# One head's value product in one slot, row sums divided out after it, and casts on GpSimd, in a bucketed attention followed by a gated convolution layer

## The chip, the cores and the metric

The kernel runs on one core of one Trainium2 chip. The core has five engines that run side by side and wait for each other through semaphores: TensorE (PE in the profile; its weight loads are PEld), VectorE (DVE), ScalarE (ACT), GpSimd (POOL), and SyncE (SP), which here only issues DMAs. The metric is the device time of one execution in microseconds (us); lower is better.

## The reference

There are B = 4 batches of H = 8 heads, each with S = 768 positions of D = 64 numbers, in float32. Every query and key gets a bucket number from the signs of six projections; a query sees only keys of its own bucket.

```python
q_bits = (einsum('bhsd,dk->bhsk', q, proj) > 0)          # six bits; the same for k
mask   = q_bucket[:, :, :, None] == k_bucket[:, :, None, :]
scores = where(mask, matmul(q, k.T) / sqrt(D), -1e9)
attn   = exp(scores - max(scores)); attn = attn / (sum(attn) + 1e-9)
x      = matmul(attn, v)                                  # heads side by side: (B, S, 512)
gate   = sigmoid(sum_k conv_w[k] * x shifted by 4-k)      # causal, five taps, per channel
out    = (gate * (x @ w_val)) @ w_out
```

`w_val`, `conv_w` and `w_out` arrive as float64, and the kernel turns their bits into float32 pairs itself.

## The kernel before, in words

**Units, tiles, slots.** A unit is one head of one batch (32 units). A tile is 128 queries of a unit against all 768 keys (6 per unit, N = 192 in all). The main loop (L453) takes one tile forward per turn; a turn is called a slot here, k. The order of every engine's instructions is written out by hand: inside `manual_schedule`, PE, ACT, DVE and POOL run exactly the order in which the loop emits them. Only SP's order of DMA issues is left to a planner. All engines are first in, first out: an instruction that waits holds everything behind it on its engine.

**Slot k.** ACT copies the transposed tile k-4 out of PSUM (`keep_transposed`, L289, two copies). DVE takes the row maxima of tile k from PSUM (L238) and makes two small factors from them (L244, L248). Between these, in every second slot, DVE adds 1e-9 to the row sums of tiles k-2 and k-1 and takes their reciprocals (L262, L266); POOL multiplies tile k-2 with them (`normalise`, L271). PE computes the scores of tile k+1 (L232, four matmuls into one of two PSUM buffers). ACT takes the exponential of tile k (L256) and adds up its rows on the way. Then come pieces of other work, each a Python generator that is moved one step at a time: `convs` (the gate's convolution), `weights` (float64 to float32 pairs, mostly DVE, over the first nine units or so), `moes` (the two matrix products of the last layer), `preps` (operands of the unit after next) and `avs` (attention times values). Last, PE transposes tile k-3 (L280; LAG = 3). A score buffer is free for tile k+2 once the exponential of tile k has read it.

**Value product.** When the sixth tile of a unit has been copied, `attn_v` is ready: 12 matmuls (six key blocks, two halves of the queries), whose 64 output columns use one half of the PE array each, so the two halves run at the same time. Every odd slot takes two steps of it, so four matmuls; the trace shows each float32 matmul as two records, so such a run is `x8`. A unit has three runs, in three slots. Its result is copied by ACT into `x` (L311). After every second head `pair_x` splits `x` into a rounded part and a rest (L323 on DVE, L324 on POOL) and runs the five taps on DVE (L332 once, L334 four times). After a batch's last pair ACT applies the sigmoid (L338) and `moe` of that batch is appended: eight `val` chunks and six `outp` chunks of three steps (four matmuls) each, two empty steps, and a `hold` before the last two `outp`, which stay until the next batch's gates are there. A `val` chunk's result is multiplied with the gate on DVE straight after its last matmul (L370) and split (L374 on DVE, L376 on POOL); an `outp` chunk's result is copied and stored (L396 or L398, L400). Both read the one PSUM buffer `m` that the next chunk fills.

**Preparation.** `prep` rounds a raw unit to fp32r on DVE (L166), POOL forms the rest (L168), and seven DMAs on SP lay out the stacked operands (L169 to L175) and load a later unit (L147); `bits` (L194, L197) makes the bucket rows for four units at a time.

Of the kernel before, what the change touches and what calls it, by code (L numbers as in the profile page):

```python
# [26 lines left out]
def kernel(  # L27
# [12 lines left out]
    P = 128  # L40
# [5 lines left out]
    LAG = 3  # L46
# [8 lines left out]
    pp = ctx.enter_context(tc.tile_pool(name="pp", bufs=LAG + 1))  # L55
# [7 lines left out]
    op = ctx.enter_context(tc.tile_pool(name="op", bufs=2))  # L63

# [92 lines left out]
    def prep(i):  # L157
# [8 lines left out]
        nc.vector.tensor_copy(out=aq, in_=r)  # L166
# [83 lines left out]
    def exponentials(k):  # L250
        s, nb = ss.pop(k), nbs.pop(k)
        p = pp.tile([P, 2, HS], FP32, name="p")
        if k % 2 == 0:
            cur["sm"] = small.tile([P, 2, 2], FP32, name="sm")
        sm = cur["sm"]
        nc.scalar.activation(out=p, in_=s[:, :, 0:HS], func=AF.Exp, bias=nb, scale=gs.pop(k), accum_out=sm[:, k % 2, 0:1])  # L256
        ps[k] = (p.rearrange("p a b -> p (a b)"), sm)


    def row_sums(k):  # L260
        sums[k] = small.tile([P, 2, 2], FP32, name="s1")
        nc.vector.tensor_scalar(out=sums[k][:, :, 0], in0=ps[k][1][:, :, 0], scalar1=1e-9, scalar2=None, op0=ALU.add)  # L262

    def recip(k):
        ri = small.tile([P, 2], FP32, name="ri")
        nc.vector.reciprocal(out=ri, in_=sums.pop(k)[:, :, 0])  # L266
        rcs[k], rcs[k + 1] = ri[:, 0:1], ri[:, 1:2]

    def normalise(k):
        p, _ = ps[k]  # L270
        nc.gpsimd.tensor_scalar(out=p, in0=p, scalar1=rcs.pop(k), scalar2=1.0, op0=ALU.mult, op1=ALU.mult)  # L271

    def transposes(k):
        p, _ = ps.pop(k)
# [19 lines left out]
    def attn_v(i, pts):  # L294
# [4 lines left out]
        for kb in range(KB):  # L299
            if kb:  # L300
                yield
            for s, pt in enumerate(pts):
                nc.tensor.matmul(out=av[s * D:(s + 1) * D, 0:HS], lhsT=vt[:, kb, hh * D:(hh + 1) * D], rhs=pt[kb // 3][:, kb % 3, :],  # L303
                                 start=(kb == 0), stop=(kb == KB - 1), tile_position=(0, s * D))
        if hh == 0:
            x = cur["x"] = xp.tile([P, S + KW - 1], FP32, name="x")
            nc.gpsimd.memset(x[:, 0:KW - 1], 0.0)
        x = cur["x"]
        for s in range(2):
            o = KW - 1 + s * HS  # L310
            nc.scalar.copy(out=x[hh * D:(hh + 1) * D, o:o + HS], in_=av[s * D:(s + 1) * D, 0:HS])  # L311
        if hh == 1:
            if c == 0:
                cur["xs"], cur["g"] = {}, []
            convs.append(pair_x(b, c, x, cur["g"], cur["xs"]))

    def pair_x(b, c, x, gs, xs_):
        for o in (0, HS):
# [4 lines left out]
            nc.vector.tensor_copy(out=xh, in_=x0)  # L323
            nc.gpsimd.tensor_tensor(out=xl, in0=x0, in1=xh.bitcast(FP32), op=ALU.subtract)  # L324
        yield
        g = gp.tile([P, S], FP32, name="g")
        gs.append(g)
        for k in range(KW):
            yield
            w = cw_sb[:, c * KW + k:c * KW + k + 1]  # L330
            if k == 0:
                nc.vector.tensor_scalar(out=g, in0=x[:, 0:S], scalar1=w, scalar2=None, op0=ALU.mult)  # L332
            else:
                nc.vector.scalar_tensor_tensor(out=g, in0=x[:, k:k + S], scalar=w, in1=g, op0=ALU.mult, op1=ALU.add)  # L334
        if c == NP - 1:
# [14 lines left out]
    def moe(b, xs_, g):  # L350
# [3 lines left out]
        def later():  # L354
            while todo:
                todo.pop(0)()

        def val(o, j):
# [11 lines left out]
            nc.vector.tensor_tensor(out=ht, in0=acc[:, 0:HS], in1=g[j][:, o:o + HS], op=ALU.mult)  # L370
# [10 lines left out]
        def outp(o, tb):  # L381
# [4 lines left out]
            for hi, wi in ((0, 0), (0, 1), (1, 0)):  # L386
# [6 lines left out]
                later()  # L393
            ob = op.tile([P, 512], FP32, name="o")
# [29 lines left out]
    raws, stacks, vts, ss, nbs, ps, tps, sums, rcs, nms, gs, cur = {}, {}, {}, {}, {}, {}, {}, {}, {}, {}, {}, {}  # L424
    avs, convs, moes = [], [], []
# [9 lines left out]

    def finish(gens):
# [120 lines left out]
```

## Time and profile before

| | before |
|---|---|
| median of 3 runs (lowest, highest) | 639.28 us (639.07, 639.45) |
| the profiled execution's own time | 637.56 us |
| its span in the trace | 635.6 us |
| granted PE clock, mean | 0.989 |
| busy: PE, DVE, ACT, POOL | 590.1, 465.9, 421.7, 364.7 us |
| main loop's last value product ends, by the chain of waits | about 589.4 us |
| first sigmoid of the gates (L338) starts | 196.3 us |

The page gives the busy time of each engine, groups of instructions with their mean duration, and the chain of work that ended last, followed backwards. On that chain a piece's length is the time by which it moved the end, which for pipelined matmuls is shorter than the duration of the record itself. A row of the stage table reads: window, its length, then busy time (and count) of PE, PEld, DVE, ACT and POOL, granted PE clock, DMA share and GB/s.

### The profile page before, as it was taken

Reading aid. Unit: us, or ns where it says so; the run is one execution under the profiler, and the core shown is the slowest. Engines: PE = TensorE matmul, PEld = TensorE weight load, DVE = VectorE, ACT = ScalarE, POOL = GpSimd, SP = SyncE. Lnnn points to the kernel's source line nnn. Section 1 sums busy time; section 2 is a strip of 40 time slices with the busy share of each in tenths; the row PEclk is TensorE's granted clock in tenths of the full one; section 3 lists DMA queues with packets and bytes.
Section 4 is the critical chain, followed back from the end, with each engine's and each line's share of the span. In section 5 each row is a group of like instructions: output and inputs, shape, how many; then the busy total and the mean of one; then the engine's idle time right before and its main releaser. Section 6 shows DMA issues by size and latency. Waiting matters only on the chain.

```text
span 635.6 us, 10630 instructions
## 1 busy us (share of the span) xinstructions
PE 590.1 (93%) x3496; PEld 424.3 (67%) x3496; DVE 465.9 (73%) x1064; ACT 421.7 (66%) x881; POOL 364.7 (57%) x326
## 2 busy tenths in 40 slices
PE   4689888878999999999999999999999999999997
PEld 2465554555567777676667877677667777776895
DVE  5789897999986766668675877578685787665532
ACT  3487776767778666667787766677778677675400
POOL 1375868577765764567653776466562677544221
PEclk9899998998999999999999999999999999999999
DMA  6533535443332334343433333343422223300111
GB/s 243 128 101 86 139 96 138 112 134 81 104 80 58 83 75 123 82 105 96 104 80 79 88 80 110 80 121 80 120 57 61 57 53 79 86 18 2 50 51 50
DMA packets 23269, 56.76 MB, mean 89 GB/s; under 512 B 4296, under 2 KB 4296, under 8 KB 23216
## 3 DMA queue, kind: packets, MB, share of 16 engines
q1 hardware_dynamic: 23072, 56.06, 32.9%
q8 instruction: 28, 0.46, 0.3%
q14 instruction: 25, 0.20, 0.1%
q10 hardware_dynamic: 144, 0.03, 0.0%
HBM read 23.12 MB, written 6.29 MB: 46 GB/s over the span
## 4 chain that ended last, share of the span: by engine, by line
PE 64%; DVE 18%; ACT 10%; issue 3%; DMA 3%; POOL 0%; DVEq 0%; ACTq 0%
PE av L303 16%; PE s L232 15%; PE tp L280 12%; PE m L390 8%; PE m L365 7%; DVE nm L238 6%; ACT p L256 4%; DVE g L334 3%; ACT pt L289 3%; ACT x L311 2%; DMA w<-in_w_out_dram 2%; DVE aq L166 1%; PE tp L365 1%; PE tp L390 1%; PE s L390 1%
## 5 line engine op out<-in xcount | busy, mean ns | idle before, releaser
L271 POOL TENSOR_SCALAR p<-p,ri 128x768 f32<-128x768 f32 x192 | 220.0, 1150 | 200.3 <-DVE nb L248 157.6
L256 ACT ACTIVATE p<-s,nb,gs 128x768 f32<-128x768 f32 x192 | 192.7, 1004 | 49.7 <-DVE nb L248 44.6
L289 ACT COPY pt<-tp 128x384 f32<-128x384 f32 x384 | 166.2, 485 | 86.0 <-PE tp L280 85.0
L238 DVE TENSOR_REDUCE nm<-s 128x1 f32<-128x768 f32 x192 | 182.4, 950 | 52.8 <-PE s L232 52.6
L280 PEld LDWEIGHTS tp<-ident,p 128*128 128x128 f32 x1152 | 130.4, 142 | 74.2 <-issue 47.3
L280 PE MATMUL tp<-ident,p 128*128 128x128 f32 x1152 | 165.4, 280 | 4.5 <-ACT pt L289 1.6
L232 PE MATMUL s<-ak,aq 76*128 76x384 f32 x384 | 118.6, 390 | 32.2 <-ACT p L256 25.4
L303 PE MATMUL av<-pt,vt 128*64 128x384 f32 x768 | 146.9, 504 | 0.0
L232 PE MATMUL s<-bk,bq 128*128 128x384 f32 x384 | 101.6, 346 | 0.0
L232 PEld LDWEIGHTS s<-ak,aq 76*128 76x128 f32 x384 | 59.4, 195 | 48.9 <-ACT p L256 39.3
L303 PEld LDWEIGHTS av<-pt,vt 128*64 128x64 f32 x768 | 47.4, 137 | 63.3 <-issue 62.7
L334 DVE SCALAR_TENSOR_TENSOR g<-x,cw_sb,g 128x768 f32<-128x768 f32 x64 | 78.4, 1225 | 0.2
L232 PEld LDWEIGHTS s<-bk,bq 128*128 128x128 f32 x384 | 71.9, 194 | 0.5 <-issue 0.5
L376 POOL TENSOR_TENSOR hl<-ht,hh 128x384 fp32r<-128x384 f32 x32 | 33.4, 1044 | 45.5 <-DVE hh L374 45.5
L168 POOL TENSOR_TENSOR bq<-r,aq 128x768 fp32r<-128x768 f32 x31 | 58.4, 1885 | 0.5 <-DVE aq L166 0.5
L311 ACT COPY x<-av 64x384 f32<-64x384 f32 x64 | 30.4, 475 | 33.5 <-PE av L303 32.9
L365 PE MATMUL m<-xh,wv 128*128 128x384 f32 x200 | 42.7, 337 | 0.0
L248 DVE TENSOR_SCALAR nb<-nm,gs 128x1 f32<-128x1 f32 x192 | 40.1, 209 | 3.5
L370 DVE TENSOR_TENSOR ht<-m,g 128x384 f32<-128x384 f32 x25 | 13.9, 555 | 35.4 <-PE m L365 32.0
L256 ACT ACTIVATION_READ_ACCUMULATOR p<-s,nb,gs 128x1 f32 x192 | 39.1, 204 | 0.0
L324 POOL TENSOR_TENSOR xl<-x,xh 128x384 fp32r<-128x384 f32 x32 | 33.5, 1066 | 9.5 <-DVE xh L323 9.5
L390 PE MATMUL m<-wo,hh 128*128 128x512 f32 x144 | 38.1, 394 | 0.0
(84 smaller groups left out, 475.6 us busy)
## 6 DMA issues: line engine op xcount, KB each, us to landing
r<-in_qk_dram SPq DMA_DIRECT2D x32, 384.0 KB
vt<-in_v_dram SPq DMA_DIRECT2D x16, 384.0 KB
out_dram<-o SPq DMA_DIRECT2D x24, 256.0 KB
ak<-aq SPq DMA_DIRECT2D x31, 192.0 KB
bk<-aq SPq DMA_DIRECT2D x31, 192.0 KB
bk<-bq SPq DMA_DIRECT2D x31, 192.0 KB
bq<-aq SPq DMA_DIRECT2D x31, 192.0 KB
w<-in_w_val_dram SPq DMA_DIRECT2D x4, 512.0 KB
```

What stands on the lines that cost most here:

```text
L168: nc.gpsimd.tensor_tensor(out=bq, in0=r, in1=aq.bitcast(FP32), op=ALU.subtract)
L232: nc.tensor.matmul(out=s[:, hf, 0:HS], lhsT=lq[0:n, qs], rhs=rk[0:n, hf * HS:(hf + 1) * HS], start=n == M, stop=n == P)
L238: nc.vector.tensor_reduce(out=nm, in_=s[:, :, 0:HS], axis=AX.XY, op=ALU.max, negate=True)
L256: nc.scalar.activation(out=p, in_=s[:, :, 0:HS], func=AF.Exp, bias=nb, scale=gs.pop(k), accum_out=sm[:, k % 2, 0:1])
L271: nc.gpsimd.tensor_scalar(out=p, in0=p, scalar1=rcs.pop(k), scalar2=1.0, op0=ALU.mult, op1=ALU.mult)
L280: nc.tensor.transpose(out=tp[:, n * P:(n + 1) * P], in_=p[:, kb * P:(kb + 1) * P], identity=ident)
L289: nc.scalar.copy(out=pt[:, :, qo:qo + P], in_=tp[:, 0:HS].rearrange("p (a b) -> p a b", b=P))
L303: nc.tensor.matmul(out=av[s * D:(s + 1) * D, 0:HS], lhsT=vt[:, kb, hh * D:(hh + 1) * D], rhs=pt[kb // 3][:, kb % 3, :], start=(kb == 0), s ...
L311: nc.scalar.copy(out=x[hh * D:(hh + 1) * D, o:o + HS], in_=av[s * D:(s + 1) * D, 0:HS])
L334: nc.vector.scalar_tensor_tensor(out=g, in0=x[:, k:k + S], scalar=w, in1=g, op0=ALU.mult, op1=ALU.add)
L365: nc.tensor.matmul(out=acc[:, 0:HS], lhsT=wv[wi][:, c, j * P:(j + 1) * P], rhs=xs_[(c, o)][xi], start=(m == 0), stop=(m == 11))
L390: nc.tensor.matmul(out=acc, lhsT=hs[(o, j)][hi][:, tb * P:(tb + 1) * P], rhs=wo[wi][:, j, :], start=(m == 0), stop=(m == 11))
```

## The change

The row sums are no longer divided out of each tile. The transposes take the raw exponentials, one slot later instead of three (LAG = 1), and POOL's `normalise` is gone. Per unit, DVE makes the six reciprocals at once, a DMA writes them to DRAM, and two DMAs read them back, each row of numbers repeated on 64 partitions (`rb`). The value product of a unit is emitted whole, in the one slot in which its last tile has been copied. Its reader, `take`, is listed in the next slot: DVE multiplies the PSUM result with `rb` into `x`, where ACT copied it before. In that whole slot `moes` is not stepped; one slot in six steps it twice instead. The convolution takes one step in the whole slot, up to four in the next one, and otherwise waits, except for a batch's last pair.

Four operations move from DVE to POOL: the rounding in `prep`, in `pair_x` and in `split`, and the first tap. The readers of the last layer's results (the gate product L370 and the output copy) go on a list `late` that is emptied behind the next slot's maximum and factors.

```diff
@@ -43,7 +43,7 @@
...
-    LAG = 3
+    LAG = 1
...
-    pp = ctx.enter_context(tc.tile_pool(name="pp", bufs=LAG + 1))
+    pp = ctx.enter_context(tc.tile_pool(name="pp", bufs=LAG + 2))
...
+    rp = ctx.enter_context(tc.tile_pool(name="rp", bufs=2))
+    dp = ctx.enter_context(tc.tile_pool(name="dp", bufs=2, space=bass.MemoryType.DRAM))
 
...
-        nc.vector.tensor_copy(out=aq, in_=r)
+        nc.gpsimd.tensor_copy(out=aq, in_=r)
...
     def exponentials(k):
         s, nb = ss.pop(k), nbs.pop(k)
         p = pp.tile([P, 2, HS], FP32, name="p")
...
-    def row_sums(k):
-        sums[k] = small.tile([P, 2, 2], FP32, name="s1")
-        nc.vector.tensor_scalar(out=sums[k][:, :, 0], in0=ps[k][1][:, :, 0], scalar1=1e-9, scalar2=None, op0=ALU.add)
-
-    def recip(k):
-        ri = small.tile([P, 2], FP32, name="ri")
-        nc.vector.reciprocal(out=ri, in_=sums.pop(k)[:, :, 0])
-        rcs[k], rcs[k + 1] = ri[:, 0:1], ri[:, 1:2]
-
-    def normalise(k):
-        p, _ = ps[k]
-        nc.gpsimd.tensor_scalar(out=p, in0=p, scalar1=rcs.pop(k), scalar2=1.0, op0=ALU.mult, op1=ALU.mult)
+        i, qt = tiles[k]
+        if qt == 0:
+            sms[i] = small.tile([P, KB], FP32, name="sm", bufs=2)
+        sm = sms[i]
+        nc.scalar.activation(out=p, in_=s[:, :, 0:HS], func=AF.Exp, bias=nb, scale=gs.pop(k), accum_out=sm[:, qt:qt + 1])
+        ps[k] = p.rearrange("p a b -> p (a b)")
+
+
+
+    def row_sums(i):
+        s1 = small.tile([P, KB], FP32, name="s1", bufs=2)
+        nc.vector.tensor_scalar(out=s1, in0=sms.pop(i), scalar1=1e-9, scalar2=None, op0=ALU.add)
+        ri = small.tile([P, KB], FP32, name="ri", bufs=2)
+        nc.vector.reciprocal(out=ri, in_=s1)
+        rows = dp.tile([2, P, KB // 2], FP32, name="rows")
+        nc.sync.dma_start(out=rows.rearrange("s p t -> p s t"), in_=ri.rearrange("p (s t) -> p s t", s=2))
+        rb = rbs[i] = rp.tile([P, P, KB // 2], FP32, name="rb")
+        for s in range(2):
+            nc.sync.dma_start(out=rb[s * D:(s + 1) * D], in_=rows[s].partition_broadcast(D))
 
...
                                  start=(kb == 0), stop=(kb == KB - 1), tile_position=(0, s * D))
+        taken.append(lambda: take(i, av))
+
+    def take(i, av):
+
+        b, h = units[i]
+        hh, c = h % 2, h // 2
         if hh == 0:
             x = cur["x"] = xp.tile([P, S + KW - 1], FP32, name="x")
             nc.gpsimd.memset(x[:, 0:KW - 1], 0.0)
-        x = cur["x"]
+        x, rb = cur["x"], rbs.pop(i)
         for s in range(2):
             o = KW - 1 + s * HS
-            nc.scalar.copy(out=x[hh * D:(hh + 1) * D, o:o + HS], in_=av[s * D:(s + 1) * D, 0:HS])
+            nc.vector.tensor_tensor(out=x[hh * D:(hh + 1) * D, o:o + HS].rearrange("d (t p) -> d t p", p=P),
+                                    in0=av[s * D:(s + 1) * D, 0:HS].rearrange("d (t p) -> d t p", p=P),
+                                    in1=rb[s * D:(s + 1) * D].rearrange("d p t -> d t p"), op=ALU.mult)
         if hh == 1:
             if c == 0:
                 cur["xs"], cur["g"] = {}, []
+            cur["last"] = c == NP - 1
             convs.append(pair_x(b, c, x, cur["g"], cur["xs"]))
 
     def pair_x(b, c, x, gs, xs_):
@@ -320,26 +332,26 @@
             xl = xs.tile([P, HS], FP32R, name="xl")
             xs_[(c, o)] = (xh, xl)
             x0 = x[:, KW - 1 + o:KW - 1 + o + HS]
-            nc.vector.tensor_copy(out=xh, in_=x0)
+            nc.gpsimd.tensor_copy(out=xh, in_=x0)
             nc.gpsimd.tensor_tensor(out=xl, in0=x0, in1=xh.bitcast(FP32), op=ALU.subtract)
-        yield
         g = gp.tile([P, S], FP32, name="g")
         gs.append(g)
...
             if k == 0:
-                nc.vector.tensor_scalar(out=g, in0=x[:, 0:S], scalar1=w, scalar2=None, op0=ALU.mult)
+                nc.gpsimd.tensor_scalar(out=g, in0=x[:, 0:S], scalar1=w, scalar2=None, op0=ALU.mult)
             else:
                 nc.vector.scalar_tensor_tensor(out=g, in0=x[:, k:k + S], scalar=w, in1=g, op0=ALU.mult, op1=ALU.add)
         if c == NP - 1:
             yield
             for g in gs:
                 nc.scalar.activation(out=g, in_=g, func=AF.Sigmoid)
-            cur["gates"] = 2
+            cur["gates"], cur["last"] = 2, False
             moes.append(moe(b, xs_, gs))
 
...
         def later():
-            while todo:
-                todo.pop(0)()
+            drain(late)
+            drain(todo)
 
         def val(o, j):
             acc = acc_tile()
@@ -367,11 +379,11 @@
                     m += 1
                 later()
             ht = hp.tile([P, HS], FP32, name="ht", bufs=2)
-            nc.vector.tensor_tensor(out=ht, in0=acc[:, 0:HS], in1=g[j][:, o:o + HS], op=ALU.mult)
+            late.append(lambda: nc.vector.tensor_tensor(out=ht, in0=acc[:, 0:HS], in1=g[j][:, o:o + HS], op=ALU.mult))
 
             def split():
                 hh = hp.tile([P, HS], FP32R, name="hh")
-                nc.vector.tensor_copy(out=hh, in_=ht)
+                nc.gpsimd.tensor_copy(out=hh, in_=ht)
                 hl = hp.tile([P, HS], FP32R, name="hl")
                 nc.gpsimd.tensor_tensor(out=hl, in0=ht, in1=hh.bitcast(FP32), op=ALU.subtract)
                 hs[(o, j)] = (hh, hl)
@@ -391,14 +403,16 @@
                                      rhs=wo[wi][:, j, :], start=(m == 0), stop=(m == 11))
                     m += 1
                 later()
+            late.append(lambda: put(o + tb * P, acc))
+            yield
+
+        def put(r0, acc):
             ob = op.tile([P, 512], FP32, name="o")
             if cur["gates"]:
                 nc.vector.tensor_copy(out=ob, in_=acc)
             else:
                 nc.scalar.copy(out=ob, in_=acc)
-            r0 = o + tb * P
             nc.sync.dma_start(out=out[b, r0:r0 + P, :], in_=ob)
-            yield
 
...
+    def drain(todo):
+        while todo:
+            todo.pop(0)()
+
     def finish(gens):
         while gens:
             step(gens)
 
-    cur["gates"], cur["end"], cur["pts"] = 0, False, []
+    cur["gates"], cur["end"], cur["pts"], cur["last"] = 0, False, [], False
     N = len(tiles)
     with tc.manual_schedule(engines=ENGINES):
         for i in range(5):
@@ -453,48 +471,50 @@
         for k in range(N + LAG + 1):
             if 0 <= k - LAG - 1:
                 keep_transposed(k - LAG - 1)
-            pair = k % 2 == 0 and 0 <= k - 2 < N
             if k < N:
                 maxima(k)
-            if pair:
-                row_sums(k - 2)
-            if k < N:
                 factors(k)
-            if pair:
-                recip(k - 2)
-            if 0 <= k - 2 < N:
-                normalise(k - 2)
-            if k < N:
                 shifts(k)
+            drain(late)
+            if 2 <= k < N + 2 and tiles[k - 2][1] == KB - 1:
+                row_sums(tiles[k - 2][0])
             if k + 1 < N:
                 if tiles[k + 1][0] != tiles[k][0]:
                     finish(preps)
+                    drain(late)
                     preps = [prep(tiles[k + 1][0] + 1)]
                 scores(k + 1)
             if k < N:
                 exponentials(k)
-            if k >= 60 or k % 2:
+            whole = bool(avs)
+            for _ in range(1 if whole or k >= N - 10 else 4 if taken else cur["last"]):
                 step(convs)
+            drain(taken)
             for _ in range((1, 0, 2, 0, 2, 2)[k % 6]):
                 step(weights[turn])
                 turn = 1 - turn
-            for _ in range(3 if cur["gates"] else 1):
+            for _ in range(0 if whole else 3 if cur["gates"] else 1):
                 step(moes)
             cur["gates"] = max(0, cur["gates"] - 1)
             step(preps)
-            if k % 2:
-                step(avs)
-                step(avs)
+            finish(avs)
             if 0 <= k - LAG < N:
                 transposes(k - LAG)
+            if k % 6 == 4 and not cur["gates"]:
+                step(moes)
         accs[:] = [(ps_m, "m"), (ps_t, "tp"), (ps_s, "s"), (ps_t, "tp"), (ps_s, "s")]
         finish(avs)
+        drain(late)
+        drain(taken)
         cur["gates"] = 0
         cur["end"] = True
         while convs:
             step(convs)
             step(moes)
-        finish(moes)
+            drain(late)
+        while moes:
+            step(moes)
+            drain(late)
 
 
 # ---- launch: one core; the arrays are only laid out anew on the host ----
```

More of the change, by code (lines that the diff above doesn't have):

```diff
@@ L252, in exponentials @@
         p = pp.tile([P, 2, HS], FP32, name="p")
[L253 to L257, printed above, removed]
-    def row_sums(k):
-        sums[k] = small.tile([P, 2, 2], FP32, name="s1")
-        nc.vector.tensor_scalar(out=sums[k][:, :, 0], in0=ps[k][1][:, :, 0], scalar1=1e-9, scalar2=None, op0=ALU.add)
-    def recip(k):
-        ri = small.tile([P, 2], FP32, name="ri")
-        nc.vector.reciprocal(out=ri, in_=sums.pop(k)[:, :, 0])
-        rcs[k], rcs[k + 1] = ri[:, 0:1], ri[:, 1:2]
-    def normalise(k):
-        p, _ = ps[k]
-        nc.gpsimd.tensor_scalar(out=p, in0=p, scalar1=rcs.pop(k), scalar2=1.0, op0=ALU.mult, op1=ALU.mult)
+        i, qt = tiles[k]
[14 more added lines that the diff above has]
+            nc.sync.dma_start(out=rb[s * D:(s + 1) * D], in_=rows[s].partition_broadcast(D))
     def transposes(k):
-        p, _ = ps.pop(k)
+        p = ps.pop(k)
         tps[k] = []
@@ L422 @@
     tiles = [(i, qt) for i in range(len(units)) for qt in range(KB)]
-    raws, stacks, vts, ss, nbs, ps, tps, sums, rcs, nms, gs, cur = {}, {}, {}, {}, {}, {}, {}, {}, {}, {}, {}, {}
-    avs, convs, moes = [], [], []
+    raws, stacks, vts, ss, nbs, ps, tps, sms, rbs, nms, gs, cur = {}, {}, {}, {}, {}, {}, {}, {}, {}, {}, {}, {}
+    avs, convs, moes, late, taken = [], [], [], [], []
     accs = [(ps_m, "m")]
@@ L496 @@
             step(moes)
-        finish(moes)
+            drain(late)
+        while moes:
+            step(moes)
+            drain(late)
 _INS = ['qk', 'v', 'proj', 'w_val', 'conv_w', 'w_out']
```

## The prediction

> **What bounds the kernel now.** I read the page's engine shares first, then the table of stages, then the chain of waits, then single engines in order of time.
>
> ```profile
> span 635.6 us, 10630 instructions
> PE 590.1 (93%) x3496; PEld 424.3 (67%) x3496; DVE 465.9 (73%) x1064; ACT 421.7 (66%) x881; POOL 364.7 (57%) x326
> ```
>
> PE looks like the bound, but 93% is a mean. The stage table for slots 6 to 47 (no work of the last layer yet) and for one batch of the middle says more; the maxima's group row gives the number of slots in each.
>
> ```profile
> 31.69:149.55 117.86, 102.14 (x621) 66.76 (x620) 106.69 (x238) 87.15 (x188) 84.05 (x73) 0.98 0.42 110
> 331.00:477.00 146.00, 143.24 (x873) 104.32 (x872) 104.91 (x250) 104.98 (x218) 85.61 (x76) 1.00 0.34 89
> L238 DVE TENSOR_REDUCE nm<-s 128x1 f32<-128x768 f32 x42 | 39.8, 948 | 6.5 <-PE s L232 6.3
> L238 DVE TENSOR_REDUCE nm<-s 128x1 f32<-128x768 f32 x48 | 45.6, 951 | 14.2 <-PE s L232 14.2
> ```
>
> Early, DVE is busiest (106.69 of 117.86, 91%); 42 slots are seven units, so a unit takes 16.84 us. In the middle PE is busy 98% (143.24 of 146.00) and 48 slots take 146.0. So **DVE sets the pace of the first eight units or so and PE that of the other 23**. How full PE is there shows on the chain:
>
> ```profile
> 376.54 0.70 PE m L365 x4
> 382.96 1.44 PE av L303 x8
> 384.40 0.81 PE tp L280 x6
> 385.21 0.70 PE s L232 x4
> 385.90 0.93 PE m L390 x4
> 386.83 0.65 PE tp L280 x6
> ```
>
> Scores 0.70, six transposes 0.65, a step of the last layer 0.70 or 0.93: a slot without a value run costs PE 1.35 bare and 2.05 to 2.28 with a step. Six transposes cost 0.81 behind a value run and 0.65 elsewhere: **leaving the two-column mode costs 0.16**. For entering it I use weight loads inside a run of 12 (that of the last unit):
>
> ```profile
> 585.72 0.15 PEld L303 LDWEIGHTS av<-pt,vt 128*64 128x64 f32 x2 [0.17 <-issue]
> ...
> 588.30 0.15 PEld L303 LDWEIGHTS av<-pt,vt 128*64 128x64 f32 x2 [0.17 <-issue]
> ```
>
> Eight steps of two records in 2.58 us are 0.3225 each. A run `x8` has four and takes 1.44, not 1.29, so entering costs 0.15.
>
> **The change part by part.** Durations are those of the profiled execution, which took 637.56 us (its span 635.6 and 1.96 around it); the median of the runs, 639.28, is 1.72 above that.
>
> *Whole value product.* Before, a unit pays 3 x (1.44 + 0.16) = 4.80; afterwards 12 x 0.3225 + 0.15 + 0.16 = 4.18. That is 0.62 less per unit. In the 23 units that PE paces: **-14.3**. In the early ones DVE hides it: 0.
>
> *Normalise, copies and casts.* These rows carry what goes and what comes:
>
> ```profile
> L271 POOL TENSOR_SCALAR p<-p,ri 128x768 f32<-128x768 f32 x192 | 220.0, 1150 | 200.3 <-DVE nb L248 157.6
> L168 POOL TENSOR_TENSOR bq<-r,aq 128x768 fp32r<-128x768 f32 x31 | 58.4, 1885 | 0.5 <-DVE aq L166 0.5
> L311 ACT COPY x<-av 64x384 f32<-64x384 f32 x64 | 30.4, 475 | 33.5 <-PE av L303 32.9
> L370 DVE TENSOR_TENSOR ht<-m,g 128x384 f32<-128x384 f32 x25 | 13.9, 555 | 35.4 <-PE m L365 32.0
> ```
>
> POOL loses 220 us and gets four casts or products. None has a POOL row. Between L271's 1.15 and L168's 1.89 for 768 columns, a unit's 768 + 384 + 384 + 384 columns cost 2.9 to 4.7 us, at most 150 in all; I take the lower, since they have one input like L271. POOL ends below 365 busy and sets no pace: 0. ACT loses 30.4, also hidden: 0. `take` is two DVE products of 384 columns, one operand in PSUM, as L370: 0.555 each; with `rb` read at a stride, up to double. Its 1.1 us matter below. The reciprocals per pair looked like a DVE saving, but they aren't:
>
> ```profile
> 97.51 0.94 DVE L238 TENSOR_REDUCE nm<-s 128x1 f32<-128x768 f32 x1
> 98.81 1.27 DVE L334 SCALAR_TENSOR_TENSOR g<-x,cw_sb,g 128x768 f32<-128x768 f32 x1
> 100.00 0.94 DVE L238 TENSOR_REDUCE nm<-s 128x1 f32<-128x768 f32 x1
> 101.05 0.17 DVE L266 RECIPROCAL ri<-s 128x2 f32<-128x2 f32 x1
> 101.30 0.42 DVE L108 CAST wo<-w 128x512 fp32r<-128x512 f32 x1
> ```
>
> From a maximum to the next piece of work are 1.30 us without them (97.51 to 98.81) and 1.30 with them (100.00 to 101.30): they sit in gaps between dependent instructions.
>
> *The way of the reciprocals.* New on the path: write to DRAM, then read back twice, all through SP, and `take` waits for it at the head of DVE's queue, with the next maximum behind it. The nearest rows are small transfers between SBUF tiles:
>
> ```profile
> 40.95 2.29 DMA ak<-u
> 305.36 0.49 SPq L169 DMA_DIRECT2D ak<-aq  x1
> ```
>
> Two hops of 2.29 and one more issue of 0.49 are an estimated 5.1 us from reciprocal to `rb`. Bounds: nothing, if `take` would not have run earlier, and 7.3 with hops half as long again. Behind the write SP holds the layout DMAs of a unit that is needed about a dozen slots later: 0. The Trainium skill (DMA: Bandwidth & Descriptors, Anatomy of one DMA) puts about 2.0 us on any DMA, most of it the receipt of the write, and calls HBM the slowest target; by it, an estimate, the way takes 4.5 us or more. No run here shows a write and read-back of this kind.
>
> *Early units.* Count from the moment at which the whole slot's scores are done. The product ends at 0.15 + 12 x 0.3225 = 4.0. The reciprocals are made at about 0.2, behind the slot's maximum, so `rb` is there at 5.3, `take` ends at 6.4. Meanwhile DVE does the next maximum and, every second unit, three taps; both end by 5. Behind `take` stand six `weights` steps and four maxima before the chain closes. Their price, seven parts in these seven units, seven steps a part:
>
> ```profile
> L100 DVE SCALAR_TENSOR_TENSOR w<-w,o 128x512 f32<-128x512 uint32 x7 | 9.0, 1279 | 0.2
> L93 DVE TENSOR_SCALAR o<-o 128x512 int32<-128x512 int32 x7 | 7.4, 1056 | 0.2
> L96 DVE SCALAR_TENSOR_TENSOR w<-w,o 128x512 int32<-128x512 int32 x7 | 5.4, 771 | 0.0
> L92 DVE TENSOR_SCALAR o<-o 128x512 f32<-128x512 f32 x7 | 3.6, 508 | 1.4 <-ACT o L90 1.4
> L99 DVE TENSOR_SCALAR o<-w 128x512 int32<-128x512 int32 x7 | 3.3, 477 | 0.0
> ```
>
> 28.7 and some 3 for the casts are 4.5 a part, 0.64 a step, 3.9 for six. Four maxima at 1.30 are 5.2. Closing the chain is an exponential and a set of scores:
>
> ```profile
> 303.14 0.99 ACT p L256 x2
> 304.18 0.96 PE s L232 x4
> 309.00 0.97 PE s L232 x4
> ```
>
> 0.99 + 0.96 and some 0.15 between are 2.1. Sum: 6.4 + 3.9 + 5.2 + 2.1 = 17.6 per unit against 16.84: **+0.8 x 8 = +6**. Ends: with `take` straight behind the product 16.4 (-4 for eight units), with the slow way 19.8 (+24). So the DVE work taken away there is paid back by DVE standing before `take`.
>
> *Last layer starts earlier.* The last pair's convolution goes on each slot, and LAG is two less: the first sigmoid moves from about slot 64 to slot 56. Eight slots before it had no last-layer step. Two such slots take 4.82 (304.18 to 309.00), PE's own work in them 2 x 1.35 + 1.60 = 4.3: 0.26 a slot wasted, now filled: **-2**.
>
> *Short slots.* Five of six slots now have no value run. With a step PE needs 2.05 or more; ACT needs an exponential and two copies, DVE 1.30 and, once in three slots, L370's 0.56 = 1.86. ACT's turn is 1.78:
>
> ```profile
> 307.85 1.01 ACT L256 ACTIVATE p<-s,nb,gs 128x768 f32<-128x768 f32 x1
> 309.63 0.99 ACT L256 ACTIVATE p<-s,nb,gs 128x768 f32<-128x768 f32 x1
> ```
>
> So PE still sets the pace. The raw transposes of tile k-1 add no wait: PE's scores just ahead of them need the same exponential, to reuse its buffer. In a batch's eight or so empty slots PE has 1.35, and ACT's 1.78 rules: 8 x 0.43 = 3.4 lost, against ten slots at 0.26 = 2.6 before: +0.8, in 2.7 batches **+2**. The moved readers (L370, the output copy) cost nothing while the buffer `m` is free again before the next chunk, one maximum later.
>
> *Loop's end.* With LAG = 1 the last tile's exponential, transposes and copies stand bare, some 2 us against about 1 before: **+1**.
>
> Sum: -14.3 + 6 - 2 + 2 + 1 = -7.3. 637.56 - 7.3 = 630.3; at the median's distance 632.0.
>
> **The rivals.**
>
> *Faster: DVE's standing is filled.* If the queue leaves `take` little to wait for, early units cost the lower end, 16.4, and where DVE is relieved of POOL's company (L334 took 1.27 above), less: 15.7. Eight units x (15.7 - 16.84) = -9 in place of +6: 617. For it: some 130 us less on POOL. Against: one long wait per unit, which is written into the order.
>
> *Slower: the reciprocals come late everywhere.* In the last-layer stretch they are made some 0.4 earlier, so `rb` is there at 4.9 and `take` ends at 6.0. The maximum behind it feeds an exponential that PE needs at about 9: 6.0 + 1.3 + 1.0 + 0.2 = 8.5, slack 0.5. The point of decision is a way of 5.6 us. At 6.3 the loss is 0.7 x 23 = 16 and early 1.2 x 8 = 10 more: 658. For it: other loads stand in the same queue. Against: the hop's row above has such company too.
>
> *No gain: the short slots lose it.* If ACT or DVE takes 2.1 to 2.15 a slot where PE needs 2.05, 5 x 0.08 x 19 units = 7.6 goes: 640. Against: the 1.78 and 1.86 above.
>
> **How the numbers follow.** Forecast 0.42 (own range 626 to 637), faster rival 0.26, late reciprocals 0.18, no gain 0.14. A measurement here can't tell less than 0.2% (1.3 us) from no change. Faster: 0.42 + 0.26 less 0.02 for the forecast's upper edge, and 0.02 of the no-gain case: 0.68. Same: 0.08. Slower: 0.24. The range holds the forecast, the faster rival and part of the late case: 612 to 648.
>
> **What would show it.** One run `x24` of value matmuls per unit, near 4.0 on the chain, and 0.65 for most transposes. DVE idle before `take`, released by a DMA: about one us a unit. Slots 6 to 47 at 17 to 18 us a unit. The first sigmoid near slot 56. PE at 98% in the middle, a batch in 141 to 143 us in place of 146. I am wrong if `take` waits two us or more, if PE waits for ACT's exponential in most short slots, or if the early units get faster.

## The result, and the profile after

The changed kernel takes 789.62 us (median of 4 runs, 786.16 to 793.01) against 639.29: ratio 1.235, 95% interval 1.228 to 1.242. The forecast was 632, at most 648; even the late rival's 658 is far off. The profiled execution took 792.63 us, its span is 790.9, its mean granted clock 0.896 (0.989 before).

The page of the changed kernel, its busy shares and the chain that ended last:

```profile
span 790.9 us, 10141 instructions
...
PE 627.9 (79%) x3496; PEld 478.7 (61%) x3496; DVE 444.3 (56%) x886; ACT 394.1 (50%) x820; POOL 238.3 (30%) x245
...
PE 30%; DMA 25%; DVE 20%; POOL 10%; ACT 8%; issue 5%; SPq 1%; DVEq 0%; ACTq 0%; POOLq 0%
```

No engine is full any more. A quarter of the chain is DMA, which had 3% of it before. The waits name it (us in total, times, longest):

```profile
DVE x L320 <- DMA rb<-rows: 139.3, 30, 11.0
...
PE s L235 <- ACT p L260: 110.2, 54, 7.5
```

And those of SP's queue:

```profile
SPq L274 <- DMA rows<-ri: 58.5, 24, 3.7
SPq L173 <- POOL bq L170: 57.8, 18, 7.0
```

`take` (L320) waits 139.3 us for the reciprocals, 4.4 a unit, and TensorE then 110.2 for exponentials. One such unit of the middle in order of time (start, duration, instruction, idle time ahead of it with what ended it):

```profile
303.25 0.19 DVE L269 RECIPROCAL ri<-s 128x6 f32<-128x6 f32 x1
...
303.85 4.09 PE L306 MATMUL av<-pt,vt 128*64 128x384 f32 x24
...
305.01 0.46 SPq L173 DMA_DIRECT2D bk<-bq  x1
...
307.59 0.47 SPq L174 DMA_DIRECT2D bq<-aq  x1
...
308.02 2.22 POOL L343 TENSOR_SCALAR g<-x,cw_sb 128x768 f32<-128x768 f32 x1
...
308.15 0.54 SPq L271 DMA_DIRECT2D rows<-ri  x1
...
310.27 3.13 DVE L345 SCALAR_TENSOR_TENSOR g<-x,cw_sb,g 128x768 f32<-128x768 f32 x3 [4.92 <-POOL x L316]
...
312.05 0.82 PE L283 MATMUL tp<-ident,p 128*128 128x128 f32 x6
...
312.45 1.11 SPq L274 DMA_DIRECT2D rb<-rows  x2
...
315.52 1.33 DVE L320 TENSOR_TENSOR x<-av,rb 64x384 f32<-64x384 f32 x2 [2.13 <-DMA rb<-rows]
...
316.88 0.96 DVE L241 TENSOR_REDUCE nm<-s 128x1 f32<-128x768 f32 x1
...
318.37 0.99 ACT L260 ACTIVATE p<-s,nb,gs 128x768 f32<-128x768 f32 x1 [6.99 <-DVE nb L251]
...
319.51 1.01 PE L235 MATMUL s<-ak,aq 76*128 76x384 f32 x2 [6.64 <-ACT p L260]
```

The reciprocals are ready at 303.44, and the write is issued at 308.15. SP's queue stands ahead of it: L173 needs POOL's `bq`, ready at 304.98, two more issues follow, and L174, which overwrites what L173 reads, waits for the end of that transfer. The write takes until 312.45, the read-back until 315.5. DVE has not stood for that alone. From 305.35 on it waits 4.92 us for the first tap, which POOL reaches only behind the casts and rests of `xh` and `xl`, then it runs the three taps until 313.40, and for the reciprocals it waits another 2.13. So it is in most units with three taps, every second one; in the others the wait for `rb` is 4.1 to 11.0 us where a DMA ends it. Only then come `take`, the next maximum, its exponential, and TensorE, which has stood still for 6.64 us. What follows runs at half clock: this pair of matmuls takes 1.01 us where the same pair ahead of the run took 0.60. Stages of 8 units early and some 9 in the middle:

```profile
29.30:207.40 178.10, 128.21 (x709) 94.72 (x707) 121.68 (x240) 93.81 (x199) 64.11 (x56) 0.82 0.38 93
400.00:600.00 200.00, 162.78 (x922) 124.25 (x919) 106.54 (x215) 105.09 (x215) 53.60 (x56) 0.91 0.33 77
```

An early unit takes 178.10 / 8 = 22.3 us instead of 16.84, and TensorE's busy share in the middle is 81% instead of 98%.

### The profile page after: what moved, and what is told of

The parts are those of the page before. It is cut to its first block, busy times and chain, and to the rows that moved or that the text cites. A ratio compares the mean times of both kernels' runs of the same rounds, so it can differ in the third digit from the quotient of the medians.

```text
span 790.9 us, 10141 instructions
## 1 busy us (share of the span) xinstructions
PE 627.9 (79%) x3496; PEld 478.7 (61%) x3496; DVE 444.3 (56%) x886; ACT 394.1 (50%) x820; POOL 238.3 (30%) x245
## 4 chain that ended last, share of the span: by engine, by line
PE 30%; DMA 25%; DVE 20%; POOL 10%; ACT 8%; issue 5%; SPq 1%; DVEq 0%; ACTq 0%; POOLq 0%
DMA rb<-rows 12%; PE s L235 9%; DMA rows<-ri 9%; DVE nm L241 7%; PE tp L283 6%; ACT p L260 5%; PE m L377 5%; DVE x L320 4%; PE av L306 4%; PE m L402 4%; POOL bq L170 3%; DMA bk<-bq 3%; DVE g L345 2%; POOL hl L388 2%; ACT pt L292 1%
## 5 line engine op out<-in xcount | busy, mean ns | idle before, releaser
L235 PE MATMUL s<-ak,aq 76*128 76x384 f32 x384 | 130.5, 424 | 115.5 <-ACT p L260 110.2
L283 PE MATMUL tp<-ident,p 128*128 128x128 f32 x1152 | 182.5, 299 | 24.8 <-DVE u L200 20.5
L283 PEld LDWEIGHTS tp<-ident,p 128*128 128x128 f32 x1152 | 151.7, 155 | 69.9 <-issue 26.7
L306 PE MATMUL av<-pt,vt 128*64 128x384 f32 x768 | 131.2, 490 | 0.0
L320 DVE TENSOR_TENSOR x<-av,rb 64x384 f32<-64x384 f32 x64 | 42.0, 656 | 151.8 <-DMA rb<-rows 139.3
L168 POOL CAST aq<-r 128x768 fp32r<-128x768 f32 x31 | 27.1, 874 | 179.2 <-PE s L235 165.5
L386 POOL CAST hh<-ht 128x384 fp32r<-128x384 f32 x32 | 16.9, 529 | 182.1 <-DVE ht L382 182.1
L377 PE MATMUL m<-xh,wv 128*128 128x384 f32 x208 | 54.8, 395 | 3.0 <-DVE ht L382 1.6
L377 PEld LDWEIGHTS m<-xh,wv 128*128 128x128 f32 x208 | 42.4, 224 | 7.2 <-DVE ht L382 4.2
L335 POOL CAST xh<-x 128x384 fp32r<-128x384 f32 x32 | 17.2, 536 | 72.5 <-DVE x L320 72.5
```

The source lines that it names most:

```text
L235: nc.tensor.matmul(out=s[:, hf, 0:HS], lhsT=lq[0:n, qs], rhs=rk[0:n, hf * HS:(hf + 1) * HS], start=n == M, stop=n == P)
L283: nc.tensor.transpose(out=tp[:, n * P:(n + 1) * P], in_=p[:, kb * P:(kb + 1) * P], identity=ident)
L320: nc.vector.tensor_tensor(out=x[hh * D:(hh + 1) * D, o:o + HS].rearrange("d (t p) -> d t p", p=P), in0=av[s * D:(s + 1) * D, 0:HS].rearran ...
L377: nc.tensor.matmul(out=acc[:, 0:HS], lhsT=wv[wi][:, c, j * P:(j + 1) * P], rhs=xs_[(c, o)][xi], start=(m == 0), stop=(m == 11))
```

## The experiments

Times are medians; the kernel before, run beside them, took 637.9 to 639.2. The expectations speak of theories. A: the reciprocals' way, with `take` at the head of DVE's queue. B: the casts and the first tap on POOL. C: the 4-us value run, too long for two score buffers. D: POOL's first tap. E: pieces of work that stand bunched on DVE, and the slots with gates. F: the list of late readers. G: the three taps in a row.

### The way and the place of `take`

The way left out (the division by the row sums is left out with it):

```diff
-        rows = dp.tile(...)   # and its three DMAs
+        rbs[i] = ones
```

> The changed kernel without the way of the reciprocals: they are still made on VectorE, but no DMA carries them, and take multiplies with a constant tile of ones (the division by the row sums is left out). Theory A (take waits for the reciprocals at the head of VectorE's queue, mean way 9.0 us against the 5.1 forecast, and everything else of the forecast stands): the 4.9 us from the product's end to take vanish, 620 to 640 us, clock back above 0.97. Theory B (POOL's new casts and first tap hold the chain): above 700 us.

Measured: **686.34**, ratio 1.075 (1.073 to 1.077): 103 us of the loss. Both expectations are missed: the way is the largest part, but not all. Part of the 103 is clock: of the 106 us between the two profiled spans 31 are TensorE's busy time (627.9 to 596.9), at a granted clock of 0.958 for 0.896.

The way kept, and issued by ACT's queue instead of SP's (the write behind the whole slot's exponential, the reads at the start of the next slot):

```diff
-        nc.sync.dma_start(out=rows..., in_=ri...)   # in row_sums
+        nc.scalar.dma_start(out=rows..., in_=ri...) # behind exponentials(k)
```

> The changed kernel with the three DMAs of the reciprocals issued by ScalarE: the write behind the exponential of the whole slot, the two reads at the start of the next slot, so that they don't stand behind the layout DMAs on SP. The wait for SP (0.0 or 3.0 to 4.7 us, mean 1.8) goes: the way falls from 9.0 to about 7 us, and 32 units x 1.8 = 58 us or somewhat more go, 715 to 740 us. If the queue of the DMA engines and not SP's order is the larger part: above 765 us.

Measured: **730.36**, 1.143 (1.140 to 1.147). As expected (715 to 740). In its trace the write is issued 0.1 us behind the reciprocals in the mean of the 32 units, 1.8 before. So some 59 of the 103 are what stands ahead on SP, 44 the rest of the way, clock included in both.

`take` listed three slots later, nothing left out, and the same with the way left out:

```diff
+        cur["due"] = cur["k"] + 4
         taken.append(lambda: take(i, av))
...
-            drain(taken)
+            if cur["due"] <= k:
+                drain(taken)
```

> The changed kernel with take listed three slots later (in the fifth slot after the row sums instead of the second); nothing left out. Theory A: with some 4 slots of 2.2 us behind the reciprocals, the way of 9 us fits and take waits under 1 us in most units: 622 to 645 us. Theory B: the POOL chain remains, above 700 us.

> take three slots later and no way of the reciprocals at all (constant ones; the division by the row sums is left out). If the way is hidden once take is three slots later: within 5 us of 666. If its DMAs still cost through SP's queue (layout operands late): 640 to 655 us.

Measured: **665.59**, 1.043 (1.040 to 1.046), and **665.0**, 1.041 (1.037 to 1.046). Three slots later the way costs nothing; A's 622 to 645 for the first is missed all the same. And 21 us more than the way itself are gone. They come from the stretch with the last layer: a batch of the middle takes 161.6 us with ones and `take` right behind the run, 153.8 with `take` later, while eight early units gain nothing (149.1 and 151.8). The kernel with ones shows a unit of the middle with three taps, on POOL, DVE and TensorE:

```profile
386.47 2.21 POOL L341 TENSOR_SCALAR g<-x,cw_sb 128x768 f32<-128x768 f32 x1
...
388.72 3.13 DVE L343 SCALAR_TENSOR_TENSOR g<-x,cw_sb,g 128x768 f32<-128x768 f32 x3 [4.90 <-POOL x L314]
...
391.76 1.30 DVE L318 TENSOR_TENSOR x<-av,ones 64x384 f32<-64x384 f32 x2
...
393.10 0.96 DVE L243 TENSOR_REDUCE nm<-s 128x1 f32<-128x768 f32 x1
...
395.73 1.01 PE L237 MATMUL s<-ak,aq 76*128 76x384 f32 x2 [4.39 <-ACT p L262]
```

The wait for POOL's first tap, the taps and `take` stand in one row ahead of the maximum; TensorE loses 4.39 us and full clock. With ones and `take` later, DVE waits 1.79 for POOL in such a unit and TensorE 0.79. So the way is shown to cost 103 us and, with its place, 124. How the 21 divide between `take` and POOL's first tap ahead of it is not shown: no run has the way left out and that tap on DVE.

### POOL

The four operations back on DVE, in the changed kernel and in the one with `take` later; and, in the kernel before, the three casts moved to POOL alone:

```diff
-        nc.gpsimd.tensor_copy(out=aq, in_=r)    # xh, hh, first tap likewise
+        nc.vector.tensor_copy(out=aq, in_=r)
```

> The changed kernel with the three casts and the first tap back on VectorE. Theory A: the way is hardly shorter, 760 to 800 us. Theory B: POOL no longer holds the layout DMAs and the taps, below 720 us.

> take three slots later, and the three casts and the first tap back on VectorE; the value product stays whole. Theory C: within 8 us of the 666 of the later take alone. Theory D: 645 to 655 us.

> The kernel before with only the three casts moved from DVE to POOL (aq, xh, hh; the first tap stays). A unit of the early stage has 0.79 of aq and 0.47 of xh less on DVE, which paces it: 8 x 1.2 = 10 us less, 629, if DVE's busy time is what counts. If POOL's order counts (the casts stand in POOL's queue among the products with the reciprocals, and xh waits there for the copy of x), it stays at 639 or gets slower, up to 646.

Measured: **784.82**, 1.230 (1.227 to 1.233); **680.34**, 1.064 (1.059 to 1.069), so 15 slower than with the operations on POOL; **635.32**, 0.994 (0.992 to 0.997). The second and the third miss both of their expectations. Theory B falls: the four operations are no loss on POOL that these runs show, and the three casts alone make the kernel before 0.6% faster. Its early units take 131.50 us for eight, 134.1 before; the middle is as before:

```profile
32.50:164.00 131.50, 115.56 (x699) 76.04 (x699) 117.11 (x255) 98.91 (x214) 106.30 (x96) 0.98 0.41 107
321.00:466.90 145.90, 143.23 (x874) 104.31 (x873) 96.38 (x227) 104.11 (x219) 98.76 (x101) 1.00 0.35 92
```

That is 2.6 of the 10 expected. DVE's busy time in these units fell by 4.8 us (121.86 to 117.11), not by 10, and the time by half of that: DVE's sum alone did not pace them.

### The long run

The whole product alone, in the kernel before; the changed kernel with three runs in three slots; and the same with `take` two slots behind the last run:

```diff
-            if k % 2:
-                step(avs)
-                step(avs)
+            finish(avs)
```

> The kernel before with one edit: the whole value product of a unit in the slot in which it becomes ready. Forecast's term (0.62 us per unit saved in 23 units that PE paces): 10 to 14 us less than before, 625 to 630 us. Rival (the short slots between are paced by ScalarE and VectorE and give it back): 636 to 650 us.

> The changed kernel with the value product back in three runs (two key blocks in each of three slots that follow each other), the last layer stepped once in every slot and the convolution as before; take comes with the third run, one slot later. Late division, LAG 1, the late list and POOL's casts stay. Theory C (the run of 4 us in one slot starves the loop of scores, maximum and exponential, which has two score buffers): 630 to 650 us, half-clock time under 25 us. Theory D (POOL's first tap and casts are what is left): no better than the 666 of the later take.

> The changed kernel, with the value product in three runs of x8 in three slots one behind the other, its reader listed two slots behind the last run, and the output copy's engine chosen when it is listed. The long run and the wait for the reciprocals are then both gone; raw transposes, reciprocals per unit, casts on POOL and the list of late readers stay. Theory C (what is left of the loss is the 4-us run, longer than the two score buffers cover): 636 to 645, near the kernel before. Theory E (what is left are DVE's bursts in the early units and the slots with gates): 650 to 660, since the bursts stay. In either case the reader of the product waits for no DMA (under 5 us in all).

Measured: **673.93**, 1.056 (1.053 to 1.059); **673.91**, 1.056 (1.053 to 1.058); **686.44**, 1.074 (1.071 to 1.077). The first and the last miss both of their expectations, and with three runs the loss is no smaller than with one (665.59), so C can't be all. Nor does the first show the long run by itself. ACT's two copies of the product stand straight behind it there, ahead of the next exponential, and ACT waits for it; that kernel's line, then that of the kernel before:

```profile
ACT x L311 <- PE av L303: 112.5, 32, 4.5
...
ACT x L311 <- PE av L303: 32.9, 30, 3.8
```

So its 36 us are the run and the place of its reader together. The last one's trace shows another place where time goes, on DVE in the slot of `take`, in order of time:

```profile
101.59 1.38 DVE L321 TENSOR_TENSOR x<-av,rb 64x384 f32<-64x384 f32 x2
...
103.00 0.80 DVE L98 SCALAR_TENSOR_TENSOR w<-w,o 128x512 int32<-128x512 int32 x1
...
103.83 0.96 DVE L241 TENSOR_REDUCE nm<-s 128x1 f32<-128x768 f32 x1
...
105.32 0.99 ACT L260 ACTIVATE p<-s,nb,gs 128x768 f32<-128x768 f32 x1 [2.96 <-DVE nb L251]
```

`take`, then a step of the weights, and only then the maximum that the exponential needs; ACT has stood for 2.96 us. Why this kernel is slower than the one with `take` straight behind the last run isn't settled.

### Bursts on DVE, and the output copy

That became theory E. With `take` later there was a second burst, on ACT: the moved output copy asks for the gates one slot later than before, and so goes to ACT, behind four sigmoids. The trace of that kernel (665.59):

```profile
349.11 0.57 ACT L415 COPY o<-m 128x512 f32<-128x512 f32 x1
...
349.73 0.99 PE L378 MATMUL m<-xh,wv 128*128 128x384 f32 x4 [2.32 <-ACT o L415]
```

So: the engine chosen at the listing, and the weights' steps moved off the slot of `take`.

```diff
-            late.append(lambda: put(o + tb * P, acc))
+            gated = cur["gates"]
+            late.append(lambda: put(o + tb * P, acc, gated))
...
-            for _ in range((1, 0, 2, 0, 2, 2)[k % 6]):
+            for _ in range((2, 0, 1, 2, 2, 0)[k % 6]):
```

> The changed kernel with the reader of the product three slots later (665.6 as measured), and two more edits: the output copy's engine is chosen when the copy is listed, so that it stays on DVE while the gates are young, and the weights' steps are moved off the slot of the reader. The whole product stays one run. Theory C (the long run is what is left): 655 to 662, the unit of the gates falls from 24.6 to about 21. Theory E (bursts and gates are what is left): 640 to 648, with the early units at 17.5.

Measured: **650.59**, 1.019 (1.016 to 1.021), between the two expectations. Early units and a batch of the middle:

```profile
31.60:169.90 138.30, 117.20 (x714) 80.37 (x712) 112.56 (x238) 91.30 (x201) 57.88 (x53) 0.98 0.47 118
339.10:490.10 151.00, 142.14 (x874) 106.91 (x873) 101.78 (x206) 96.34 (x204) 56.10 (x56) 1.00 0.39 100
```

138.30 / 8 = 17.3 a unit, where the prediction had 17.6. Without these two edits the same stretches took 151.80 and 153.80. The early units have no work of the last layer, so most of the 15 us are the weights' steps; the two edits were not tried apart.

### The list of late readers

Alone in the kernel before (output copy by the gates at the listing), and taken out of the 650.59 kernel:

> The kernel before with only the readers of the last layer's results listed behind the next slot's maximum (the output copy's engine is chosen when it is listed). As forecast for this part: 0, so 638 to 640. If the readers come so late that PE waits for the buffer m, each chunk of 14 a batch loses up to 0.5 us: 28 us, 667 at most.

> The 650.6 kernel (whole product, its reader three slots later, output copy by the gates, weights' steps moved), with the readers of the last layer's results straight behind their matmuls again, as in the kernel before. Theory F (the list of late readers costs here what it cost the kernel before alone, 8.2 us): 641 to 644. Theory C (the long run is what is left): 648 to 652, no change.

Measured: **647.36**, 1.013 (1.010 to 1.016), and **649.99**, 1.018 (1.015 to 1.020). The list costs the kernel before 8 us, between its two expectations, and the changed one nothing; theory F falls.

### What is left

The 649.99 kernel with three runs again; with the convolution's steps spread; the same with the first tap on DVE:

```diff
-            for _ in range(1 if whole or k >= N - 10 else 4 if taken and k == cur["due"] - 3 else cur["last"]):
+            if cur["last"] or k >= N - 10 or 1 <= k % 6 <= 4:
                 step(convs)
```

> As the run with the readers straight behind their matmuls, and the value product in three runs of x8 in three slots one behind the other, one convolution step in each of them, a last-layer step in every slot, and the weights' steps spread so that the reader's slot has none. TensorE has 23 x 0.62 = 14 us more of its own work again. Theory C (the long run starves ACT and the two score buffers): the waits of TensorE for exponentials fall by more than that, 632 to 640. If the long run costs nothing: 650 to 660.

> As the 650.0 kernel (whole product, reader three slots later, readers of the last layer straight behind their matmuls), with the convolution's steps one a slot, in the whole slot and the three behind it, in place of one and then three at once; the weights' steps one or two a slot with none in the reader's slot. Theory G (three taps at once behind POOL's first tap hold the next maximum by 3 to 4 us, of which TensorE loses about one, once a pair, and more in the early units): 636 to 643, and the early units near 16.8. If the bunch costs nothing: 648 to 652.

> As the run with the steps spread, with the first tap on DVE again. Theory G: the same within 3 us, since POOL's first tap then has a slot of its own before the second tap needs it. Theory D (the first tap on POOL, 2.2 us against 0.8 on DVE, is late by itself): 4 to 8 us less than with the steps spread alone.

Measured: **659.58**, 1.029 (1.020 to 1.037; its runs lie between 650.5 and 661.9), eight early units 131.3, eight of the middle 157.1, where the 649.99 kernel has 140.0 and 150.6; **668.29**, 1.045 (1.040 to 1.051), far above both expectations; **666.73**, 1.044 (1.039 to 1.049), within G's 3 us. C's 632 to 640 is missed: what three runs gain early they lose in the middle. D falls. Spreading moved a batch's sigmoids into the whole slot, and TensorE waits inside the value run for a copy behind them, then goes on at half clock:

```profile
350.33 5.78 PE L306 MATMUL av<-pt,vt 128*64 128x384 f32 x22 [2.76 <-ACT pt L292]
```

So the steps were spread from slot 60 on only, without a batch's last pair; and then the product was cut into three runs below slot 60:

```diff
+            if 60 <= k < N - 10 and not cur["last"]:
+                n = 1 <= k % 6 <= 4
...
-            finish(avs)
+            step(avs)
+            step(avs)
+            if k >= 60:
+                finish(avs)
```

> As the 650.0 kernel, with the convolution's steps one a slot from slot 60 on, but a batch's last pair as there (so the sigmoids stay out of the whole slot), and the early units untouched. Theory G (the bunch of three taps is part of what is left): 3.5 us less in each of 2.7 batches, so 639 to 643, and a batch of the middle in 147 in place of 150.6. If the bunch costs nothing: 649 to 651.

> As the run with the steps spread from slot 60 on, and below slot 60 the value product in three runs of x8 in three slots, with one step of the convolution in each and one or two steps of the weights a slot, none in the reader's. In the run with three runs everywhere the eight early units took 131.3 in place of 139.9. If that came from the early units' own order: 8 us under the run before this, 631 to 635. If not: the same as it.

Measured: **647.79**, 1.015 (1.013 to 1.017), and **639.58**, 1.003 (1.001 to 1.006). The last kernel's stages:

```profile
29.90:159.50 129.60, 117.36 (x713) 78.05 (x712) 112.12 (x239) 92.31 (x200) 56.63 (x53) 0.97 0.50 126
334.60:482.90 148.30, 141.95 (x874) 106.93 (x873) 100.22 (x206) 97.06 (x204) 54.62 (x56) 1.00 0.40 99
```

Both miss their ranges. Theory G is not shown. A batch falls from 150.6 to 148.3, two thirds of what was forecast for it, but the whole kernel only from 649.99 to 647.79, where 9 us were forecast, and the two intervals overlap. In the early units the other order gains more, 129.60 against 140.7, part of which the slots behind give back; the early product, its reader, the taps and the weights' steps moved there together, so their shares stay open. The late division, LAG = 1 and POOL's four operations are in this last kernel, the whole product from slot 60 on, the list of late readers no longer; it is where the kernel before was. What is left in the middle, 148.3 against 146.0 with less work on TensorE, stays open: the raw transposes and `take` on DVE were not tried alone. One candidate, not tested, is ACT: its copies of a transposed tile stand ahead of the next exponential, and in the 649.99 kernel they wait 142.0 us in all for the transposes, 85.0 before.

## Why the prediction was wrong

**The step that failed** is in the way of the reciprocals: "Behind the write SP holds the layout DMAs of a unit that is needed about a dozen slots later: 0". What is queued behind the write was priced, not what stands ahead of it. SP reaches the write only when it is through with what stands ahead, above all L173, which needs POOL's `bq`, and L174: 4.7 us in the unit shown, 1.8 in the mean of the 32, so 59 in all, about what moving the way to ACT's queue gave. The hops were too small as well: the reads are issued 3.5 after the write in the mean, where 2.29 was taken, and from the second read's issue to `take` are another 3.1 (2.29). From the reciprocal to `take` it is 9.0 us, not 5.1, and outside the 7.3 that was the upper bound; of the 3.9 the queue is 1.8, the hops are 2.1. In the first eight units, with 8.4, the queue is only 0.3. The Trainium skill's figure (DMA: Bandwidth & Descriptors, Anatomy of one DMA), by which the way had 4.5, an estimate, is fitted there to DMAs that GpSimd issues; here SP issues them, and the part behind SP, 308.15 to 315.52, is 7.4. The measurement decides.

**A second step failed** in the count of the early units, "three taps; both end by 5". It has no wait for the first tap on POOL. In the unit shown, one of the middle, the taps end 9.5 us behind the whole slot's scores (303.92 to 313.40), since POOL's first tap comes late; over the kernel DVE waits for it nine times, 33.6 us in all.

**The mechanism was the late rival's**, with a chance of 0.18, and its price failed too. Its point of decision, 5.6, was passed by 3.4, where it priced 0.7, and it had no term for the clock. With the same 3496 matmuls TensorE is busy 627.9 us here and 584.8 in the 650.59 kernel, whose clock is 0.992: 43 us, the gaps' second price. 3.4 us in 31 units would be 105, close to the 103 that went with the way, but by luck: 31 of those are clock. The runs give the account in this order, clock included in each step: 789.6, less 103 for the way, 21 for its place, 15 for the weights' steps and the output copy, is 650.6. What is left to the forecast's 632 lies in the middle, 151.0 a batch for 141 to 143.

**Whole product, -14.3:** right as TensorE's own work. The chain of the 650.59 kernel has the run and the six transposes behind it:

```profile
380.01 4.02 PE av L306 x24
384.03 0.81 PE tp L283 x6
```

4.02 + 0.16 = 4.18, as forecast. But it is no gain in time: with that batch of the middle in 148.3 at best (forecast 141 to 143), waits took back more than it gave. "The 23 units that PE paces" were read from an order made for three short runs; the whole product, with ACT's reader straight behind it, cost that kernel 36 us.

**Early units, 17.6:** in the changed kernel it was 22.3. 17.3 came out with `take` three slots later and the weights' steps elsewhere, in another order on DVE than the sum counts; that the two agree is luck and no test of the sum.

**Casts on POOL, 0:** right for POOL's busy time, 238.3 us, and the three casts are better than 0 where alone (-4). What it left out is the delay of the first tap, above. No single price lay in its bounds by columns: the casts were below (874 ns for 768, some 530 for 384), the first tap with 2.21 above. The sum, 97 us, is near the lower bound, 2.9 x 32 = 93, because the two errors are opposite, which is luck:

```profile
L343 POOL TENSOR_SCALAR g<-x,cw_sb 128x768 f32<-128x768 f32 x16 | 35.4, 2210 | 0.0
L168 POOL CAST aq<-r 128x768 fp32r<-128x768 f32 x31 | 27.1, 874 | 179.2 <-PE s L235 165.5 <-ACT pt L292 13.6
```

`take` is 0.656 an instruction for 0.555: 0.2 a unit, no matter.

**Moved readers, 0:** wrong where alone (+8); taken out of the 650.59 kernel it changed nothing. What the step missed is the output copy: by asking for the gates a slot later it changed its engine, and TensorE waited 4.6 us for it in the 665.59 kernel.

**Short slots (+2), last layer earlier (-2), loop's end (+1):** the first sigmoid came in slot 56, as forecast. The two other sizes are below what these runs can part from the rest. Of what would show the forecast wrong, "`take` waits two us or more" came true on the page at once; PE waits for ACT's exponential 54 times in 192 slots, which is not "in most short slots".

## What to carry to other kernels

A reader that waits for a DMA at the head of an in-order queue is priced by everything ahead of that DMA on its own queue, waits included, and then by every instruction behind the reader; listing it some slots later cost nothing here and was worth 124 us. A gap on TensorE of some three us can have a second price, as here, the half clock that follows. And work saved on the engine that is full is time saved only as long as the others can still feed it: try the part alone first, since one small part of this change was faster, by 0.6%, and the whole was not.

## What had not been expected of the hardware

The granted clock. In the changed kernel the trace records it at half for 166.7 us, in 25 stretches, nearly all of 3.4, 6.8 or 10.2 us (before: 14.5 us, in four). In the kernel with the steps spread, 22 of the 24 records of a value run took 5.78 us, 3.4 of them at half clock, where 4.09 is usual for all 24. The Trainium skill (TensorE: Matmul & The Clock Gate, What's actually happening) has half rate follow an idle window of about 3.4 us; the trace agrees in the step of the lengths, and shows it too behind a gap shorter than that (2.76 in its row above). The prediction's sum had no term for it.
